# Linear attention with expert routing: subtracting the queries' maxima one round earlier, and three small reorderings

## The chip, the cores and the metric

The kernel runs on one core of one Trainium2 chip. Its time is the device time of one execution in microseconds (us), given as the median of three executions. A profiled execution gives the trace from which every row below is taken; its times are counted from its first instruction. Engines are written as in the profile: PE is TensorE, PEld its weight loads, DVE is VectorE, ACT is ScalarE, POOL is GpSimd, SP is SyncE, which here issues most DMA transfers.

## The reference

Three blocks follow one another: linear attention, a mixture of eight experts with one expert per token, and a dense block.

```python
proj = x @ w_phi                                    # x is q or k: 4 batches, 8 heads, 576 rows, 64 wide
proj = proj - max(abs(proj), axis=-1)               # 128 features
phi  = concat(exp(proj), exp(-proj))
kv   = einsum('bhsf,bhsd->bhfd', phi(k), v);  z = phi(k).sum(over s)
attn = (phi(q) @ kv) / (phi(q) @ z + 1e-6)          # then to x: 2304 tokens x 512

e    = argmax(normalised(x) @ normalised(expert_emb).T / tau)
x    = gate[e] * (relu(x @ w1[e]) @ w2[e])          # experts 512 -> 1024 -> 512

h    = max(x @ m1, x @ m2, x @ m3)                  # 512 -> 768
out  = h @ w_out                                    # 2304 x 512
```

All is float32.

## The kernel before, in words

The order of the work on every engine is the order in which the code is written; an engine takes its instructions strictly one after the other and waits where one of them lacks its input or its buffer.

**Attention** (function `attention`) goes in 18 rounds, r0 to r17, and a tail. Keys come in 18 steps of up to 256 rows of four heads; queries in 16 portions v (half a batch's rows, four heads each, two units u of two heads per portion). A round holds pieces of several of them, each at another stage:

- `q_front(v)`: PE projects the queries of a portion into `psqf` (L331), ACT copies them to `pq` (L335), POOL takes the maximum over the 128 partitions, `partition_all_reduce`, into `mq` (L337). Two units, so two of each; POOL's is called PAR below.
- `q_exp(u)`: DVE subtracts `mq` from `pq` (L341), ACT takes the two exponentials into `ex` (L343, L344). It belongs to the portion of the round before.
- `k_proj`, `k_T`, `k_exp` for the next key step: products into `pskp` (L212), transposes into `pskT` with ACT's copy `kT` (L203), then per half DVE's maximum `mk` (L223) and subtraction `pk` (L225) and ACT's two exponentials `kp` (L226, L227).
- `q_T`: transposes of a later portion (`psqT`), DVE's copies `qT` (L319).
- `xwork`: for finished tokens, transposes `psxd` (L388) and `psx` (L405) and DVE's scaling `x` (L418).
- `k_acc`: products with the values into `kv` (L264), and the sums `z` (L269), which for a full step take `zr`, DVE's sum of two halves of `kp` made by `k_pair` (L236) at the end of the round before. `k_fin` closes a batch (`kvT` L276, `psz` L287, `pskv` L300).
- `q_num`, `q_den`: numerators `psn` (L363) and denominators `psd` (L378), DVE's copy `dn` (L380).

PSUM banks for the products and transposes come from one pool of five, handed out in turn (`bank`): a transpose late in a round waits until the reader of an earlier tile, for example DVE's `pk` or ACT's `kT`, has let its bank go. Portion v is projected in round r1 for v = 0 to r8 for v = 7, and in r10 to r17 for v = 8 to 15; r9 has no `q_front`.

**The tail** computes the routing: `Routing.blocks` makes one-hot rows `R` in three groups (L647), PE turns them into the token list `rt_tok` (L704), DVE copies it to `s2t` (L715), and POOL gathers the tokens of the first expert block from `x_d` by it (L868). The last rows of `x_d` are scaled and stored in between (`x_put`, L418 and L419). Two products per group keep PE at work (`warm`, L657).

**The experts** (`Moe`) and **the dense block** (`Moe2`) come after; no line of theirs is changed.

Of the kernel before, what the change touches and what calls it, by code (L numbers as in the profile page):

```python
# [11 lines left out]
I32 = mybir.dt.int32  # L12
AF = mybir.ActivationFunctionType
ALU = mybir.AluOpType
# [32 lines left out]
def attention(tc, q, k, v, w_phi, expert_emb, tau, x_d, lraw, ssq, ident, io, late, rt, ids):  # L47
# [6 lines left out]
    nc = tc.nc  # L54
    B, H, S, D = q.shape
    NF = w_phi.shape[1]
    E = expert_emb.shape[0]
    P = 128
    NT = B * S // P
    NP_ = H // 2  # L60
    SH = S // 2
    QR = SH // 4
    DH = D // 2
    NV = 4 * B
    LEAD = 4

    with ExitStack() as ctx:
# [67 lines left out]
        w2 = cp.tile([P, NF], F32, tag="w2", name="w2")  # L135
# [96 lines left out]
        def k_pair(n):  # L232

            if n < NS and steps[n][2] is not None:
                zr[n] = wk.tile([P, 4, 2 * NF], F32, tag="zr", name=f"zr{n}", bufs=1)
                nc.vector.tensor_tensor(zr[n], kp[n][:, :, 0], kp[n][:, :, 1], op=ALU.add)  # L236
# [69 lines left out]
        qT, pq, mq, ex, ot, dn, xs = {}, {}, {}, {}, {}, {}, {}  # L306
# [14 lines left out]
        def q_front(v):  # L321

            m, g = divmod(v, 2)
            for pp in range(2):
                u = m * NP_ + 2 * g + pp
                d = wk.tile([P, 2, SH], F32, tag="pq", name=f"pq{u}", bufs=4)
                psb = [bank(f"psqf{u}_{a}")[:, 0:SH] for a in range(2)]
                for j in range(2):
                    for a in range(2):
                        x = slice(a * D, (a + 1) * D)  # L330
                        nc.tensor.matmul(psb[a][:, j * 2 * QR:(j + 1) * 2 * QR], w2[x],  # L331
                                         qT[v][x, 2 * pp + j].rearrange("p b s -> p (b s)"), start=True, stop=True)
                dv = d.rearrange("p j (b a s) -> p j b a s", b=2, a=2)
                for a in range(2):
                    nc.scalar.copy(dv[:, :, :, a, :], psb[a].rearrange("p (j b s) -> p j b s", j=2, b=2))  # L335
                mx = wk.tile([P, 2, SH], F32, tag="mq", name=f"mq{u}", bufs=3)
                nc.gpsimd.partition_all_reduce(mx.rearrange("p a b -> p (a b)"), d.rearrange("p a b -> p (a b)"), P, ReduceOp.absmax)  # L337
                pq[u], mq[u] = d, mx

        def q_exp(u):  # L340
            nc.vector.tensor_tensor(pq[u], pq[u], mq.pop(u), op=ALU.subtract)  # L341
            e = wk.tile([P, 2, 2, SH], F32, tag="ex", name=f"ex{u}", bufs=10)
            nc.scalar.activation(e[:, 0], pq[u], AF.Exp)  # L343
            nc.scalar.activation(e[:, 1], pq[u], AF.Exp, scale=-1.0)  # L344
            ex[u] = e
# [91 lines left out]
        for b in range(B):  # L437
            lst = [pc for pc in pcs if pc[1] == b]
            for i, (n, bb, lo, hi) in enumerate(lst):
                r = max(n, done.get(b - 1, n))  # L440
# [5 lines left out]
        at = {r: qd for qd, r in back.items()}  # L446
# [23 lines left out]
        k_proj(0)  # L470
        for _ in k_exp(0):
            pass
        k_pair(0)
        fin = None
        for r in range(R1):

            if r + LEAD in at:
                q_front(at[r + LEAD])
            if r + LEAD - 1 in at:
                m, g = divmod(at[r + LEAD - 1], 2)  # L480
                for pp in range(2):
                    q_exp(m * NP_ + 2 * g + pp)
            k_proj(r + 1)

            k_T(r + 2)
            ke = k_exp(r + 1)
            next(ke, None)
            if r and r + LEAD + 1 in at:
                q_T(at[r + LEAD + 1])
            for _ in ke:  # L490
                pass
            if fin is not None:
                for _ in fin:
                    pass
                fin = None
            if xwork:
                if next(xwork[0], "end") == "end":
                    xwork.pop(0)
                    if xwork:
                        next(xwork[0])  # L500
            for _ in pe if r == 2 else ():
                pass

            pl = work.get(r, [])
            ends = [pc[1] for pc in pl if pc[5]]
            for pc in pl:
                if not ends or pc[1] == ends[0]:
                    k_acc(*pc)
            if r < NS:
                load_next(r)  # L510
            if ends:
                fin = k_fin(ends[0])
                next(fin)
            if r in at:
                m, g = divmod(at[r], 2)
                for pp in range(2):
                    q_num(m * NP_ + 2 * g + pp)
                if fin is not None:
                    next(fin)
                if g == 1:  # L520
                    q_den(m)
                    xwork.append(tiles(m))
            elif fin is not None:
                next(fin)
            for pc in pl:
                if ends and pc[1] != ends[0]:
                    k_acc(*pc)
            k_pair(r + 1)
            if r == 0:
                q_T(at[LEAD + 1])  # L530
            if r == 7:
                rt.token_ids(ids, QR)
            if r == R1 - 3:
                late(1)
            if r == R1 - 1:
                late(3)
# [22 lines left out]
        chain = rt.blocks(lambda nm: ps1.tile([P, free[0][1]], F32, tag=free.pop(0)[0], name=nm), bank)  # L559
# [7 lines left out]
        next(chain)  # L567
        xb = [(t, rv, x_out(t)) for t, rv in rb]
        x_put(*xb[0], act=True, dma=nc.scalar, sq=False)
        for x in xb[1:]:  # L570
            next(chain)
            x_put(*x, dma=nc.sync, sq=False)
        for _ in chain:
            pass
        for t in tb:
# [13 lines left out]
class Routing:  # L589
# [83 lines left out]
    def blocks(self, bank, wbank):  # L673

        nc, gp, rp, P, NT, E, NB = self.nc, self.gp, self.rp, 128, self.NT, self.E, self.NB
        V = nc.vector
        pet = [P, E, NT]
        t_ = lambda shape, nm, dt=F32: self.tmp(rp, shape, nm, dt)
        oh = self.oh
        inc = self.inc = self.tmp(gp, pet, "inc")  # L680
        V.tensor_tensor_scan(inc.rearrange("p e t -> p (e t)"), self.d0.rearrange("p e t -> p (e t)"),
                             oh.rearrange("p e t -> p (e t)"), 0.0, op0=ALU.mult, op1=ALU.add)
        ps = bank("rt_n")
        nc.tensor.matmul(ps[:, 0:E], self.ones, inc[:, :, NT - 1], start=True, stop=True)
        ps2 = bank("rt_before")
        nc.tensor.matmul(ps2[:, 0:E], self.tri, inc[:, :, NT - 1], start=True, stop=True)
        yield

        nb = t_([P, E], "nb")
        V.tensor_scalar(nb, ps[:, 0:E], 1.0, (P - 1) / 2, op0=ALU.max, op1=ALU.add)  # L690
        V.tensor_scalar(nb, nb, ROUND * P, -ROUND * P, op0=ALU.add, op1=ALU.add)
        cb = self.cb
        V.tensor_tensor_scan(cb[:, 1:], self.o8, nb, 0.0, op0=ALU.mult, op1=ALU.add)
        self.pos = self.places(rp, gp, cb, ps2[:, 0:E], "b")
        rf, bf = self.rows(rp, self.pos, "b")
        ohb = t_([P, NT, NB + 1], "ohb", F32R)
        full = [P, NT, NB + 1]
        V.tensor_tensor(ohb, bf.unsqueeze(2).to_broadcast(full), self.jb.unsqueeze(1).to_broadcast(full), op=ALU.is_equal)
        V.tensor_tensor(ohb, ohb.bitcast(F32), self.tid.unsqueeze(2).to_broadcast(full), op=ALU.mult)

        ps3 = bank("rt_tok")
        for group in self.one_hots(rp, rf, "R", (6, 6, 6)):
            for t, R in group:
                nc.tensor.matmul(ps3[:, 0:NB + 1], R, ohb[:, t, :], start=(t == 0), stop=(t == NT - 1))  # L704
            if t < NT - 1:
                self.warm(wbank, WARM[3])
            yield

        eb = t_([1, NB, E], "eb")
        V.tensor_tensor(eb, self.jb[0:1, 0:NB].unsqueeze(2).to_broadcast([1, NB, E]),  # L710
                        cb[0:1, 1:].unsqueeze(1).to_broadcast([1, NB, E]), op=ALU.is_ge)
        ebs = t_([1, NB], "ebs")
        V.tensor_reduce(ebs, eb, axis=AX.X, op=ALU.add)
        self.s2t = self.tmp(gp, [P, NB], "s2t", I32)
        V.tensor_copy(self.s2t, ps3[:, 0:NB])  # L715

        self.before = self.tmp(gp, [P, E], "before")
        V.tensor_copy(self.before, ps2[:, 0:E])
        ne = t_([P, E], "ne")
        V.tensor_copy(ne, ps[:, 0:E])  # L720
        self.ebi = self.tmp(gp, [1, NB], "ebi", I32)
        V.tensor_scalar(self.ebi, ebs, float(E - 1), None, op0=ALU.min)
        self.nbi = self.tmp(gp, [1, 1], "nbi", I32)
        V.tensor_scalar(self.nbi, cb[0:1, E:E + 1], 1.0 / P, None, op0=ALU.mult)
        V.tensor_tensor_scan(self.cn[:, 1:], self.o8, ne, 0.0, op0=ALU.mult, op1=ALU.add)
        yield
# [567 lines left out]
```

## Time and profile before

| | us |
|---|---|
| median of 3 runs | 824.07 (823.74 to 824.57) |
| profiled execution, time | 823.43 |
| its span, first to last instruction | 821.5 |
| PE busy | 780.2 (95%) |
| DVE busy | 520.5 (63%) |
| ACT busy | 450.2 (55%) |
| POOL busy | 162.6 (20%) |

The profiled execution's time is its span and 1.9 us around it. Attention and its tail take the first 222 us; the first expert block starts its products near 229 us, and from 260 us on PE is busy nearly without a break. So a microsecond saved ahead of 222 us is a microsecond of the whole, if the end of attention moves with it. Busy shares alone hide what happens inside a round, since every engine works on each round for a part of it: there one reads which instruction each engine waits for, and what ended the wait.

### The profile page before, as it was taken

The numbers are of one execution on the slowest core, as the hardware profiler recorded it, in microseconds if no ns is written. First come the engines' busy times: TensorE is split into PE (matmuls) and PEld (weight loads), VectorE is DVE, ScalarE is ACT, GpSimd is POOL, SyncE is SP. The second block draws the span as 40 slices with busy tenths as digits, with TensorE's granted clock in tenths as the row PEclk, the third lists the DMA queues.
The fourth block names the chain that finished last, engine by engine and source line by source line (L and its number), as shares of the span: only waits on it lengthen the run. The fifth ranks groups of instructions, "written<-read, shape, count | busy, mean of one in ns | idle before, by whom it ended". The sixth has DMA issues, their size and how long they took to land. (4 is left out here: it accounts for less than half of the span.)

```text
span 821.5 us, 14129 instructions
## 1 busy us (share of the span) xinstructions
PE 780.2 (95%) x5617; PEld 655.3 (80%) x5617; DVE 520.5 (63%) x673; ACT 450.2 (55%) x622; POOL 162.6 (20%) x117
## 2 busy tenths in 40 slices
PE   6889898889899999999999999999999999999996
PEld 4656565655678888888888787999989999899984
DVE  7666666766799999999888897888212222122210
ACT  3676656666678888888887895454221112211111
POOL 2554223442151121110332021000130002200001
PEclk9899999999999999999999999999999999999999
DMA  8534432025234347534654543452121001200001
GB/s 200 122 84 105 108 91 73 15 79 201 74 104 169 122 150 276 214 141 161 228 187 153 206 142 104 160 177 75 38 81 36 1 1 39 77 1 1 0 26 52
DMA packets 61988, 87.82 MB, mean 107 GB/s; under 512 B 9488, under 2 KB 39832, under 8 KB 61920
## 3 DMA queue, kind: packets, MB, share of 16 engines
q1 hardware_dynamic: 53392, 64.51, 24.7%
q0 software_dynamic: 4880, 15.99, 5.9%
q10 hardware_dynamic: 3648, 6.38, 2.1%
q8 instruction: 46, 0.75, 0.4%
q14 instruction: 22, 0.18, 0.1%
HBM read 129.59 MB, written 16.00 MB: 177 GB/s over the span
## 5 line engine op out<-in xcount | busy, mean ns | idle before, releaser
L898 DVE TENSOR_TENSOR wL<-raw,wH 128x2048 fp32r<-128x2048 f32 x88 | 200.0, 2289 | 21.3 <-ACT wH L897 20.6
L897 ACT CAST wH<-raw 128x2048 fp32r<-128x2048 f32 x88 | 167.6, 1916 | 29.4 <-PE ph L924 12.9
L1125 PE MATMUL ps<-yH,m2WH 128*128 128x384 f32 x432 | 145.1, 336 | 1.3 <-ACTq L1261 1.3
L1125 PE MATMUL ps<-yH,m2WL 128*128 128x384 f32 x432 | 145.0, 336 | 0.0
L1125 PE MATMUL ps<-yL,m2WH 128*128 128x384 f32 x432 | 145.0, 336 | 0.0
L337 POOL PARTITION_ALL_REDUCE mq<-pq x32 | 71.3, 2274 | 109.2 <-ACT pq L335 109.2
L1125 PEld LDWEIGHTS ps<-yH,m2WH 128*128 128x128 f32 x432 | 81.2, 188 | 1.8 <-ACTq L1261 1.7
L1133 ACT CAST h2H<-mm 128x384 fp32r<-128x384 f32 x36 | 18.5, 515 | 115.6 <-DVE mm L1130 115.6
L1125 PEld LDWEIGHTS ps<-yL,m2WH 128*128 128x128 f32 x432 | 81.2, 188 | 0.1
L1125 PEld LDWEIGHTS ps<-yH,m2WL 128*128 128x128 f32 x432 | 81.2, 188 | 0.0
L1079 POOL DMA_INDIRECT yg<-ys,c2s x18 | 24.8, 1378 | 247.4 <-PE psyT L1094 222.6
L868 POOL DMA_INDIRECT xs<-x_d,s2t x22 | 42.3, 1923 | 153.5 <-PE psxT L907 90.1
L956 PE MATMUL py<-wH,hH 128*128 128x512 f32 x176 | 70.4, 400 | 0.4 <-ACT hH L942 0.4
L956 PE MATMUL py<-wH,hL 128*128 128x512 f32 x176 | 69.2, 393 | 0.1
L956 PE MATMUL py<-wL,hH 128*128 128x512 f32 x176 | 68.8, 391 | 0.0
L1129 DVE TENSOR_TENSOR mm<-mm,ps 128x384 f32<-128x384 f32 x36 | 19.9, 553 | 74.5 <-PE ps L1125 74.3
L924 PE MATMUL ph<-wH,xH 128*128 128x512 f32 x176 | 56.5, 402 | 0.7 <-ACT xH L910 0.7
L924 PE MATMUL ph<-wH,xL 128*128 128x512 f32 x176 | 54.7, 392 | 0.2 <-DVE xL L911 0.2
L924 PE MATMUL ph<-wL,xH 128*128 128x512 f32 x176 | 54.5, 391 | 0.0
L1130 DVE TENSOR_TENSOR mm<-mm,ps 128x384 f32<-128x384 f32 x36 | 20.0, 555 | 43.4 <-PE ps L1125 43.4
L1147 ACT ACTIVATE ot<-pso,gatec 128x512 f32<-128x512 f32 x18 | 12.4, 689 | 60.2 <-PE pso L1145 32.9
L1148 POOL DMA_INDIRECT out_dram<-ot,c2t x18 | 17.7, 983 | 132.3 <-ACT ot L1147 128.6
(214 smaller groups left out, 1428.3 us busy)
## 6 DMA issues: line engine op xcount, KB each, us to landing
raw<-in_moe_w_dram SPq DMA_DIRECT2D x88, 1024.0 KB
wr<-in_moe_w_dram SPq DMA_DIRECT2D x18, 512.0 KB
ys<-y ACTq DMA_DIRECT2D x22, 256.0 KB
q<-in_q_dram SPq DMA_DIRECT2D x8, 576.0 KB
kv<-in_v_dram SPq DMA_DIRECT2D x8, 512.0 KB
x_d<-x SPq DMA_DIRECT2D x16, 256.0 KB
kv<-in_k_dram SPq DMA_DIRECT2D x7, 512.0 KB
wr<-in_moe_w_out_dram SPq DMA_DIRECT2D x6, 512.0 KB
```

What stands on the lines that cost most here:

```text
L337: nc.gpsimd.partition_all_reduce(mx.rearrange("p a b -> p (a b)"), d.rearrange("p a b -> p (a b)"), P, ReduceOp.absmax)
L868: nc.gpsimd.indirect_dma_start(out=d, out_offset=None, in_=self.x_d, in_offset=bass.IndirectOffsetOnAxis(ap=self.s2t[:, j:j + 1], axis=0))
L897: nc.scalar.copy(wH, ex.raw[i])
L898: nc.vector.tensor_tensor(wL, ex.raw[i], wH.bitcast(F32), op=ALU.subtract)
L924: nc.tensor.matmul(ph[:, n * 512:(n + 1) * 512], a[:, cs], w[:, c * DF + n * 512:c * DF + (n + 1) * 512], start=(kc == 0 and f == 0), stop ...
L956: nc.tensor.matmul(py, a[:, cs], w[:, ws], start=(fc == 0 and q == 0), stop=(fc == 7 and q == 2))
L1079: self.nc.gpsimd.indirect_dma_start(out=d, out_offset=None, in_=self.ys[0:rows, :], in_offset=bass.IndirectOffsetOnAxis(ap=self.rt.c2s[:, ...
L1125: nc.tensor.matmul(ps, w[:, c], y[:, k], start=(k == 0 and q == 0), stop=(k == NK - 1 and q == 2))
L1129: nc.vector.tensor_tensor(m, m, pss[1], op=ALU.max)
L1130: nc.vector.tensor_tensor(m, m, pss[2], op=ALU.max)
L1133: nc.scalar.copy(hH[:, f], m)
L1148: nc.gpsimd.indirect_dma_start(out=self.out, out_offset=bass.IndirectOffsetOnAxis(ap=self.rt.c2t[:, t:t + 1], axis=0), in_=o, in_offset=None)
```

## The change

- The subtraction of the maxima leaves `q_exp` and becomes `q_sub(v)`. It runs in the round that projected the portion, behind that round's `k_exp`, `fin` and `xwork`, instead of at the head of the next round.
- `k_pair(0)`, which stood ahead of the rounds, runs in r0 behind `k_exp(1)`; and in r0 the `q_T` of the first portion now comes ahead of `k_pair(1)`.
- In `q_front`, two products of 144 columns per array half and unit become one of 288.
- In the tail, all three one-hot groups come ahead of the second `x_put`, the copy to `s2t` comes ahead of the third, and the two products that only kept PE at work between the groups go.

```diff
-                for j in range(2):
-                    for a in range(2):
-                        x = slice(a * D, (a + 1) * D)
-                        nc.tensor.matmul(psb[a][:, j * 2 * QR:(j + 1) * 2 * QR], w2[x],
-                                         qT[v][x, 2 * pp + j].rearrange("p b s -> p (b s)"), start=True, stop=True)
+                for a in range(2):
+                    x = slice(a * D, (a + 1) * D)
+                    nc.tensor.matmul(psb[a], w2[x], qT[v][x, 2 * pp:2 * pp + 2].rearrange("p j b s -> p (j b s)"),
+                                     start=True, stop=True)
...
+        def q_sub(v):
+            m, g = divmod(v, 2)
+            for pp in range(2):
+                u = m * NP_ + 2 * g + pp
+                nc.vector.tensor_tensor(pq[u], pq[u], mq.pop(u), op=ALU.subtract)
+
         def q_exp(u):
-            nc.vector.tensor_tensor(pq[u], pq[u], mq.pop(u), op=ALU.subtract)
...
-        k_pair(0)
         fin = None
         for r in range(R1):
...
             for _ in pe if r == 2 else ():
                 pass
+            if r == 0:
+                k_pair(0)
+            if r + LEAD in at:
+                q_sub(at[r + LEAD])
...
-            k_pair(r + 1)
             if r == 0:
                 q_T(at[LEAD + 1])
+            k_pair(r + 1)
...
-        for x in xb[1:]:
-            next(chain)
-            x_put(*x, dma=nc.sync, sq=False)
+        next(chain)
+        next(chain)
+        x_put(*xb[1], dma=nc.sync, sq=False)
+        next(chain)
+        x_put(*xb[2], dma=nc.sync, sq=False)
...
-            if t < NT - 1:
-                self.warm(wbank, WARM[3])
             yield
+        self.s2t = self.tmp(gp, [P, NB], "s2t", I32)
+        V.tensor_copy(self.s2t, ps3[:, 0:NB])
+        yield
...
-        self.s2t = self.tmp(gp, [P, NB], "s2t", I32)
-        V.tensor_copy(self.s2t, ps3[:, 0:NB])
```

On DVE at the start, from the second half of key step 0 to the end of r0. Before:

```order
L223 TENSOR_REDUCE mk_1_224<-pskp_1_208 128x4
L225 TENSOR_TENSOR pk_1_226<-pskp_1_208,mk_1_224 128x512
L236 TENSOR_TENSOR zr_230<-kp_217 128x1024
L223 TENSOR_REDUCE mk_0_250<-pskp_0_232 128x4
L225 TENSOR_TENSOR pk_0_252<-pskp_0_232,mk_0_250 128x512
L223 TENSOR_REDUCE mk_1_256<-pskp_1_233 128x4
L225 TENSOR_TENSOR pk_1_258<-pskp_1_233,mk_1_256 128x512
L236 TENSOR_TENSOR zr_285<-kp_249 128x1024
L319 COPY qT_289<-psqT_0_290 128x4x72
L319 COPY qT_289<-psqT_1_296 128x4x72
```

The same place in the changed kernel:

```order
L223 TENSOR_REDUCE mk_1_224<-pskp_1_208 128x4
L225 TENSOR_TENSOR pk_1_226<-pskp_1_208,mk_1_224 128x512
L223 TENSOR_REDUCE mk_0_248<-pskp_0_230 128x4
L225 TENSOR_TENSOR pk_0_250<-pskp_0_230,mk_0_248 128x512
L223 TENSOR_REDUCE mk_1_254<-pskp_1_231 128x4
L225 TENSOR_TENSOR pk_1_256<-pskp_1_231,mk_1_254 128x512
L236 TENSOR_TENSOR zr_260<-kp_217 128x1024
L319 COPY qT_287<-psqT_0_288 128x4x72
L319 COPY qT_287<-psqT_1_294 128x4x72
L236 TENSOR_TENSOR zr_300<-kp_247 128x1024
```

The first pair sum stands behind the maxima and subtractions of step 1, and the second behind the copies of the first queries.

On DVE where r6 passes into r7 (`dn` is the copy of r6's denominators, the last `mk` belongs to r7). Before:

```order
L225 TENSOR_TENSOR pk_1_938<-pskp_1_898,mk_1_936 128x512
L380 COPY dn_991<-psd_992 128x288
L236 TENSOR_TENSOR zr_1010<-kp_914 128x1024
L341 TENSOR_TENSOR pq_867<-pq_867,mq_876 128x576
L341 TENSOR_TENSOR pq_878<-pq_878,mq_887 128x576
L223 TENSOR_REDUCE mk_0_1060<-pskp_0_1042 128x4
```

The same place in the changed kernel:

```order
L225 TENSOR_TENSOR pk_1_914<-pskp_1_874,mk_1_912 128x512
L343 TENSOR_TENSOR pq_849<-pq_849,mq_856 128x576
L343 TENSOR_TENSOR pq_858<-pq_858,mq_865 128x576
L384 COPY dn_969<-psd_970 128x288
L236 TENSOR_TENSOR zr_988<-kp_890 128x1024
L223 TENSOR_REDUCE mk_0_1032<-pskp_0_1014 128x4
```

The two subtractions of a portion have moved ahead of `dn` and `zr`, and nothing stands between `zr` and the next round's `mk` any more.

On PE, the queries' projection of one round (r7). Before:

```order
L331 MATMUL psqf_0_1013<-qT_923,w_85 128x144
L331 MATMUL psqf_1_1014<-qT_923,w_85 128x144
L331 MATMUL psqf_0_1013<-qT_923,w_85 128x144
L331 MATMUL psqf_1_1014<-qT_923,w_85 128x144
L331 MATMUL psqf_0_1024<-qT_923,w_85 128x144
L331 MATMUL psqf_1_1025<-qT_923,w_85 128x144
L331 MATMUL psqf_0_1024<-qT_923,w_85 128x144
L331 MATMUL psqf_1_1025<-qT_923,w_85 128x144
```

The same place in the changed kernel:

```order
L330 MATMUL psqf_0_991<-qT_899,w_85 128x288
L330 MATMUL psqf_1_992<-qT_899,w_85 128x288
L330 MATMUL psqf_0_1000<-qT_899,w_85 128x288
L330 MATMUL psqf_1_1001<-qT_899,w_85 128x288
L212 MATMUL pskp_0_1014<-w_85,kT_888 128x128
```

Four products of twice the columns stand for eight, with the first product of the next key step behind them; the two array halves still take turns.

## Rows read from the trace of the kernel before

**Rows 1.** Stretch totals: length, busy us (instructions) per engine, granted clock, DMA.

```profile
260.00:820.00 560.00, 550.55 (x2883) 494.18 (x2881) 334.27 (x323) 279.59 (x289) 70.79 (x51) 1.00 0.30 106
```

**Rows 2.** Stretch totals of the four stretches at a granted clock of 0.50.

```profile
20.04:23.45 3.41, 3.41 (x30) 3.41 (x32) 0.00 (x0) 1.40 (x4) 1.25 (x1) 0.50 0.95 212
33.69:37.10 3.41, 3.41 (x32) 1.78 (x36) 2.12 (x6) 2.99 (x6) 0.49 (x1) 0.50 0.39 79
125.85:129.26 3.41, 3.13 (x22) 1.80 (x26) 3.27 (x11) 2.83 (x6) 1.16 (x1) 0.50 0.00 0
183.88:187.29 3.41, 3.41 (x36) 1.70 (x32) 2.38 (x8) 1.88 (x4) 0.00 (x0) 0.50 0.03 11
```

**Rows 3.** Timeline, r0 into r1: start, us, engine, line, names, count, [idle before].

```profile
12.84 1.23 DVE L236 TENSOR_TENSOR zr<-kp 128x1024 f32<-128x1024 f32 x1 [1.22 <-ACT kp L227]
...
13.98 0.68 DVE L223 TENSOR_REDUCE mk<-pskp 128x4 f32<-128x512 f32 x1
...
15.29 1.22 PE L317 MATMUL psqT<-ident,q 72*128 72x72 f32 x8
15.31 0.68 DVE L223 TENSOR_REDUCE mk<-pskp 128x4 f32<-128x512 f32 x1
...
20.03 2.29 PE L331 MATMUL psqf<-qT,w 64*128 64x144 f32 x16 [3.52 <-DVE qT L319]
```

**Rows 4.** Timeline of r2, from the maxima to PE's wait.

```profile
29.16 5.02 POOL L337 PARTITION_ALL_REDUCE mq<-pq  x2 [2.65 <-ACT pq L335]
29.66 2.52 DVE L341 TENSOR_TENSOR pq<-pq,mq 128x576 f32<-128x576 f32 x2
...
33.65 0.54 PE L183 MATMUL ps_en<-ident,emb 8*128 8x8 f32 x4 [2.58 <-DVE pk L225]
```

**Rows 5.** Timeline of r4, PE's two waits.

```profile
46.76 1.16 PE L212 MATMUL pskp<-w,kT 64*128 64x128 f32 x14 [0.98 <-ACT pq L335]
...
53.16 1.02 PE L280 MATMUL z<-kvT,enp 128*32 128x256 f32 x8 [1.42 <-ACT kvT L276]
```

**Rows 6.** Timeline of r5, where no subtraction delays the round's head.

```profile
56.83 1.25 PE L331 MATMUL psqf<-qT,w 64*128 64x144 f32 x16
58.49 4.26 POOL L337 PARTITION_ALL_REDUCE mq<-pq  x2 [7.13 <-ACT pq L335]
...
60.70 0.41 PE L287 MATMUL psz<-ident,zs 128*128 128x128 f32 x2 [0.30 <-DVE pk L225]
...
61.83 1.09 PE L300 MATMUL pskv<-ident,kvT 128*128 128x128 f32 x8 [0.72 <-ACT kT L203]
```

**Rows 7.** Timeline of r7.

```profile
76.76 1.25 PE L331 MATMUL psqf<-qT,w 64*128 64x144 f32 x16
78.41 2.52 DVE L341 TENSOR_TENSOR pq<-pq,mq 128x576 f32<-128x576 f32 x2
82.40 0.41 PE L388 MATMUL psxd<-ident,dn 128*128 128x128 f32 x2 [2.07 <-DVE pk L225]
82.74 0.66 PE L405 MATMUL psx<-ident,oT 128*128 128x128 f32 x4
```

**Rows 8.** Timeline of r9, the round without a projection.

```profile
100.34 1.42 DVE L341 TENSOR_TENSOR pq<-pq,mq 128x576 f32<-128x576 f32 x2
...
103.23 0.41 PE L287 MATMUL psz<-ident,zs 128*128 128x128 f32 x2 [2.26 <-DVE pk L225]
```

**Rows 9.** Timeline of r11 and r16.

```profile
126.13 0.66 PE L388 MATMUL psxd<-ident,dn 128*128 128x128 f32 x2 [2.09 <-DVE pk L225]
...
177.04 1.25 PE L331 MATMUL psqf<-qT,w 64*128 64x144 f32 x16
...
182.68 0.63 PE L405 MATMUL psx<-ident,oT 128*128 128x128 f32 x4 [2.29 <-DVE pk L225]
```

**Rows 10.** Timeline of the hand-over to the experts.

```profile
219.62 0.68 DVE L418 TENSOR_TENSOR x<-psx,r 128x512 f32<-128x512 f32 x1
...
223.52 1.30 POOL L868 DMA_INDIRECT xs<-x_d,s2t  x1 [28.44 <-issue]
```

## The prediction

> **What bounds the kernel now.** I read the totals by stretch first. From 260 us to 820 PE is busy 550.55 of 560 us [rows 1]: nothing of the change lies there, and what attention and its tail lose ahead of 222 us is lost to the whole. Then I read the timeline of attention round by round, looking only for idle time in front of a PE instruction and for what ended it. A round with nothing in its way is r5: its projection starts at 56.83, the first transpose that needs a bank from DVE at 60.70, with 0.30 of idle, the one that needs ACT's `kT` bank at 61.83 [rows 6]. So a clean round has these two at +3.87 and +5.00. Against it the reader is to see three places. In r2, r7, r9, r11 and r16 the same kind of transpose waits 2.07 to 2.58 us for DVE's `pk` [rows 4, 7 to 9]. In each of these rounds the two subtractions of the queries' maxima stand ahead of the round's `mk` and `pk` on DVE; in r2 and r7 they also run beside POOL's PAR and take 2.52 instead of 1.42 us [rows 4, 7, 8]. At the start, PE idles 3.52 us before the first projection [rows 3]. And four stretches of 3.41 us have a granted clock of 0.50, that is 1.2 GHz [rows 2]; PE idled in front of each of them, by 3.52, 2.58, 2.09 and 2.29 us [rows 3, 4, 9].
>
> **The change part by part.**
>
> *First pair sums.* Before, DVE sits idle for 1.22 us, from 11.62, because `zr` of step 0 at 12.84 waits for ACT, and step 1's maxima stand behind it [rows 3]. Now step 1's two pairs of maximum and subtraction start at 11.62; a pair takes 15.31 - 13.98 = 1.33 us, two 2.7, and `zr` follows from 14.3 to 15.5 instead of 12.84 to 14.07. PE's `z` waits for it, so `psqT` behind `z` moves by the same 1.4, from 15.29 to 16.7 at the latest, and ends with its 1.22 us near 17.9 [rows 3]. DVE copies it at once, since the second `zr` no longer stands ahead of the copies, and the projection starts near 18.1 instead of 20.03. Gain 1.9. Bounds: 0, if the first queries or the later `z` hold all behind them; 3.5, if the whole idle goes.
>
> *Subtractions earlier.* They are the same 32 instructions, now queued in the round of their PAR. In a clean round PAR ends at 58.49 + 4.26 = 62.75, that is +5.92 [rows 6]; DVE has two `mk`, two `pk` and two `qT` copies to do until about then, so the first subtraction waits little. Behind the waiting instruction stand only `dn`, `zs` and `zr`, wanted by PE no sooner than the next round. So the move costs nothing as long as DVE has about 1.5 us to spare at the end of a round; without that cover it would cost up to the pair's 1.42 us per round. What goes, each a wait of PE:
> - r2: 2.58 of idle to the clean 0.30, gain 2.3.
> - r4: 0.98 for ACT's `pq` and 1.42 for `kvT` [rows 5], both because ACT runs late after exponentials that waited for the subtractions. ACT has little to spare in these short rounds, so I take 1.0; bounds 0 and 2.4.
> - r7: the first transpose could start at 76.76 + 3.87 = 80.63 instead of 82.40, but next is `psx`, which waits for ACT's `kT` bank: 76.76 + 5.00 = 81.76 instead of 82.74 [rows 6, 7]. Gain 1.0, not 1.8: ACT is late next.
> - r9: 100.34 loses its 1.42 us pair, less the overlap of some 0.1; gain 1.3 [rows 8].
> - r11 repeats r7 (2.09 for 2.07): 1.0 [rows 9].
> - r16 has no `kT`, so the transpose itself counts: 177.04 + 3.87 = 180.91 instead of 182.68 [rows 6, 9], gain 1.8.
> - The other rounds are clean already; nothing. Sum of the six: 8.4.
>
> *The clock.* With the idle in front of the four slow stretches gone or shortened I expect the full clock there. The prices: the first projection took 2.29 us, a clean one 1.25 [rows 3, 7], 1.0. The other three cost at most half of PE's busy time in them: 1.7, 1.6 and 1.7 [rows 2]. I take 1.4, 1.3 and 1.6, a little less, since PE had to wait for other engines in them too. Sum 5.3; bounds 0 (slow stretches fall elsewhere instead) and 6.0 (1.0 and the three halves).
>
> *One product per half.* Columns are the same: per unit and half 2 x 144 against 288. The eight products of a round stand as 16 instructions in 1.25 us [rows 7]; now eight, with half the weight loads, which lie beside the products anyway. I take 0. Bounds: +0.15 per round saved, 2.4 in 16 rounds, if an eighth of the 1.25 is cost per instruction; a loss of 1.0 per round, 16 in all, if the halves stopped overlapping.
>
> *Tail.* The last `x_put` started at 219.62 and the gather at 223.52, after that row had been stored [rows 10]. The `R` group ahead of it now comes earlier, but it also stands behind `s2t`, which waits for PE's token list. I take 0.3 earlier; bounds -0.5 and 1.0. Fewer products that only keep PE at work could cost clock at the hand-over, at most half of a stretch like those in [rows 2], 1.7.
>
> *Sum.* 1.9 + 8.4 + 5.3 + 0 + 0.3 = 15.9. The profiled execution took 823.43, 1.9 around its span of 821.5, so 807.5 for an execution like it. The median of the runs is 0.64 above that execution: 808.2.
>
> **Rivals.**
>
> *The clock is not given back.* The waits go, but slow stretches come elsewhere in attention, whose PE remains idle here and there. For it: r7 and r9 idled as long (2.07, 2.26) without one, so where they fall is not fixed by the wait alone [rows 7, 8]. Against it: after the change no wait over about 1.5 us is left between r1 and r17. 808.2 + 5.3 = 813.5.
>
> *The first rounds are bound by everything at once.* r1 to r4 are the shortest rounds, and PAR, DVE and ACT each have a full portion and a full key step in them; with the waits gone, `zr` slips into the next PAR and ACT runs late. Then r0, r2 and r4 give nothing (1.9 + 2.3 + 1.0), nor does the clock in r1 and r2 (2.4): 808.2 + 7.6 = 815.8. Against it: each of these waits has one named cause that the change takes away.
>
> *The halves stop overlapping.* 16 us of loss: 824.2, no change. Against it: a product already stands as two instructions on one half, and the halves take turns as before.
>
> *Every round's subtraction meets its PAR* (slower). The pair took 2.52 instead of 1.42 where it met a PAR, and that pair of PARs 5.02 instead of 4.26 [rows 4, 6, 8]: 1.10 + 0.76 = 1.86 us. If DVE came to the subtraction with PAR still running in all 16 rounds and had no slack, 16 x 1.86 = 29.8 would come on top: 808.2 + 29.8 = 838.0; it makes the kernel measurably slower from 1.1 us per round on, (825.7 - 808.2) / 16. For it: at +5.92 PAR ends just as DVE arrives. Against it: what is left of PAR then is a few tenths, and in rounds with `xwork` DVE arrives later still.
>
> The Trainium skill, SBUF — State Buffer, section "Who interferes with whom", says that a DVE instruction with two SBUF inputs contends with a GpSimd instruction that reads SBUF, and that the one which issues second is blocked for the whole of the other. By that rule a subtraction that comes early would wait for all of what is left of a PAR of 2.13 us, 16 x 2.13 = 34 us at most and a time of 842 at the far end. The trace agrees that they contend, but has 1.10 us for the delay, not 2.13 [rows 4, 8].
>
> **How the numbers follow.** Forecast, with the clock given back in most places: 0.62, own range 804.5 to 812. Clock not given back: 0.15. First rounds give nothing: 0.13. Halves: 0.05. Collisions: 0.05. A range from 804.5 to 815.5 takes in the forecast with what may still come on top (the merged products' 2.4, 1.0 of the tail), the clock rival and, nearly, the first rounds' case, and leaves out the last two and the far ends of the terms. About 0.2%, 1.6 us, is what a measurement of this kernel can tell from no change. Faster by more than that: 0.91. Within: 0.04, most of the halves' case. Slower: 0.05.
>
> **What would show it.** In the changed profile: the first projection near 18 us; r2 without an idle of over 0.5 in front of `ps_en`; the first transposes of r7, r11 and r16 near +3.9 and `psx` waiting for ACT's `kT`; every pair of subtractions near 1.5 us and none at 2.5; a granted clock of 1.00 where the four stretches stood; r5's start near 49 instead of 56.83; attention's end some 15 us earlier and from there to the end the same length as before. It is wrong if the eight projection instructions of a round take over 1.4 us, if `zr` makes PE wait in r1 to r4, or if as many slow stretches remain as there were.

## The result, and the profile after

The changed kernel takes 811.17 us (median of four executions, 809.54 to 815.09), the kernel before, beside it on the same chip, 824.32 (823.74 to 824.65). The ratio is 0.9848 with a 95% interval of 0.9812 to 0.9884, a gain of 13.2 us where 15.9 were forecast. The profiled execution took 811.43 with a span of 809.4, 12.0 and 12.1 less than before. The two traces run 11.7 us apart from the first expert's products on, and 12.1 from 483.0 us of the kernel before on: 0.4 of the 12.1 comes at one step inside the experts (481.6 to 483.0), and the trace of attention and its tail must hold the 11.7.

The timeline of the changed kernel first, in the places of [rows 3 to 10]. Columns: start, us, engine, line, operation, names, count, and in brackets the idle time before it and what ended that. The subtraction is now L343, the projection L330.

```profile
15.24 0.89 PE L269 MATMUL z<-zr,ones 128*32 128x256 f32 x8 [1.76 <-DVE zr L236]
...
17.84 2.29 PE L330 MATMUL psqf<-qT,w 64*128 64x288 f32 x8 [0.55 <-DVE qT L319]
25.25 1.42 DVE L343 TENSOR_TENSOR pq<-pq,mq 128x576 f32<-128x576 f32 x2
...
25.40 1.24 PE L330 MATMUL psqf<-qT,w 64*128 64x288 f32 x8
29.41 0.38 PE L183 MATMUL ps_en<-ident,emb 8*128 8x8 f32 x4 [0.30 <-DVE pk L225]
...
45.75 1.44 PE L280 MATMUL z<-kvT,enp 128*32 128x256 f32 x8 [1.42 <-ACT kvT L276]
47.12 3.64 PE L264 MATMUL kv<-kp,vr 64*32 64x256 f32 x32
...
73.24 1.24 PE L330 MATMUL psqf<-qT,w 64*128 64x288 f32 x8
77.11 0.41 PE L392 MATMUL psxd<-ident,dn 128*128 128x128 f32 x2 [0.30 <-DVE pk L225]
78.23 0.66 PE L409 MATMUL psx<-ident,oT 128*128 128x128 f32 x4 [0.71 <-ACT kT L203]
...
99.34 0.66 PE L409 MATMUL psx<-ident,oT 128*128 128x128 f32 x4 [0.74 <-DVE pk L225]
...
168.83 1.24 PE L330 MATMUL psqf<-qT,w 64*128 64x288 f32 x8
172.69 0.63 PE L409 MATMUL psx<-ident,oT 128*128 128x128 f32 x4 [0.52 <-DVE pk L225]
...
181.32 1.86 DVE L343 TENSOR_TENSOR pq<-pq,mq 128x576 f32<-128x576 f32 x1 [1.27 <-POOL mq L336]
183.44 0.76 DVE L343 TENSOR_TENSOR pq<-pq,mq 128x576 f32<-128x576 f32 x1 [0.27 <-POOL mq L336]
...
207.98 0.68 DVE L422 TENSOR_TENSOR x<-psx,r 128x512 f32<-128x512 f32 x1
211.87 1.30 POOL L876 DMA_INDIRECT xs<-x_d,s2t  x1 [28.47 <-issue]
```

Every wait for DVE's `pk` of over 2 us is gone: r2's idle is 0.30 instead of 2.58, r7's transpose starts at +3.87 and `psx` behind it waits for ACT's `kT` at +4.99, r9 has no such wait left for `psz` and only 0.74 for a `psx`, r16's stands at +3.86. Fifteen of the 16 pairs of subtractions take 1.41 to 1.44 us; the last, in r17, waits for its PAR and runs beside it, 1.86 and 0.76. Two things are new. At the start PE now waits 1.76 us for `zr` ahead of `z`, where it did not wait before. In r4 the wait for `kvT` is the 1.42 us it was [rows 5], but the 32 products behind it take 3.64 us, where the same products in a round at full clock take 1.93.

The stretch totals of the changed kernel say why. Columns: stretch and length, then busy us (instructions) of PE, PEld, DVE, ACT and POOL, the granted clock, DMA share and GB/s.

```profile
15.50:22.33 6.83, 6.28 (x43) 4.86 (x36) 2.51 (x4) 1.40 (x4) 2.30 (x2) 0.50 0.97 231
...
46.22:49.63 3.41, 3.41 (x30) 1.26 (x32) 1.56 (x2) 0.00 (x0) 0.00 (x0) 0.50 0.03 5
49.63:53.04 3.41, 3.41 (x32) 1.48 (x25) 0.00 (x0) 0.00 (x0) 0.00 (x0) 0.50 0.00 0
53.04:56.46 3.42, 3.42 (x25) 2.92 (x22) 0.04 (x1) 2.37 (x6) 1.84 (x1) 0.50 0.00 0
...
210.06:213.47 3.41, 3.41 (x18) 3.41 (x18) 0.51 (x1) 2.56 (x4) 1.30 (x2) 0.50 0.04 16
```

The kernel before had two such stretches beside the four of [rows 2]:

```profile
13.21:16.62 3.41, 3.30 (x32) 1.55 (x23) 3.34 (x5) 1.22 (x3) 1.44 (x4) 0.50 0.88 158
221.42:224.84 3.42, 3.42 (x17) 3.42 (x18) 0.24 (x1) 2.82 (x4) 1.30 (x1) 0.50 0.13 50
```

From 33.69, 125.85 and 183.88, where slow stretches stood [rows 2], the clock is now 1.00. But the one at the start is as long as the two that stood there together (13.21 and 20.04), and there is a new one of 10.24 us in r4 and r5, in which PE is busy all the time. Before the experts the trace before had 20.5 us at half rate, six stretches of 3.41 or 3.42 us; the trace after has 6.83 + 10.24 + 3.41 = 20.5 as well.

The starts of the projections, read from the timelines of both kernels, put the gain into rounds (r8 and r9 together, since r9 has no projection; rounds that differ by 0.01 or less are left out):

| round | length before | length after | gain | forecast, wait + clock |
|---|---|---|---|---|
| start to r1's projection | 20.03 | 17.84 | 2.19 | 1.9 |
| r1 | 7.10 | 7.56 | -0.46 | 0 + 1.0 |
| r2 | 10.73 | 6.61 | 4.12 | 2.3 + 1.4 |
| r3 | 6.11 | 5.77 | 0.34 | 0 |
| r4 | 12.86 | 14.61 | -1.75 | 1.0 |
| r5 | 10.26 | 11.19 | -0.93 | 0 |
| r7 | 10.81 | 9.81 | 1.00 | 1.0 |
| r8 and r9 | 22.44 | 21.11 | 1.33 | 1.3 |
| r11 | 12.13 | 9.80 | 2.33 | 1.0 + 1.3 |
| r16 | 12.12 | 8.66 | 3.46 | 1.8 + 1.6 |
| r17 to the first expert's transpose | 38.33 | 38.28 | 0.05 | 0.3 |

They add up to 11.7. All rows but those of r1, r4 and r5, where the clock went down, come within 0.5 of the forecast.

### The profile page after: what moved, and what is told of

The parts are those of the page before. It is cut to its first block, busy times and chain, and to the rows that moved or that the text cites. A ratio compares the mean times of both kernels' runs of the same rounds, so it can differ in the third digit from the quotient of the medians.

```text
span 809.4 us, 13863 instructions
## 1 busy us (share of the span) xinstructions
PE 778.3 (96%) x5485; PEld 651.4 (80%) x5485; DVE 516.1 (64%) x673; ACT 448.9 (55%) x622; POOL 162.1 (20%) x117
## 5 line engine op out<-in xcount | busy, mean ns | idle before, releaser
L336 POOL PARTITION_ALL_REDUCE mq<-pq x32 | 69.1, 2207 | 101.0 <-ACT pq L334 101.0
```

## The experiments

Each of e1 to e4 makes one part of the change alone in the kernel before (824.68 us beside them, 29 executions).

**e1, the subtractions alone.**

```
+        def q_sub(v): ...                       # as in the change
         def q_exp(u):
-            nc.vector.tensor_tensor(pq[u], pq[u], mq.pop(u), op=ALU.subtract)
...
             for _ in pe if r == 2 else ():
                 pass
+            if r + LEAD in at:
+                q_sub(at[r + LEAD])
```

> The kernel before with the subtractions of the maxima moved to the end of their round, and nothing else. Theory (each wait of PE for pk in r2, r7, r9, r11, r16 came from the subtractions in front of it; the half-rate stretches only move): the waits go as in the changed kernel, 8.4 us, and the slow stretches stay about as long in sum as before: 816, between 813 and 818, with psxd of r7 at +3.9 after the projection. Rival (the full clock comes back with the waits, so another part of the change brought the slow stretch of r4 and r5): 811.6. Rival (the subtraction gains only together with the earlier start of r1): over 820.

812.35 us, ratio 0.9864 (0.9831 to 0.9896). Nearly the whole gain is in this part. The theory's 816 missed and the first rival's price, 811.6, came: e1 gains 12.3 us, 3.9 more than the forecast for the waits. Its profiled execution has 10.24 us at half rate before the experts, not 20.5, and its six executions have a mean clock of 0.987 on average against 0.981 for the kernel before beside them, so part of the clock seems to have come back with the waits. That another part of the change brings the slow stretch in r4, as the rival has it, doesn't follow; e12 below has all the parts and no such stretch in its trace. The profiled execution, mean clock 0.991, has no slow stretch in r4 either, though the wait there is the same; the rows are PE's of r4:

```profile
40.60 1.25 PE L331 MATMUL psqf<-qT,w 64*128 64x144 f32 x16
...
48.57 1.02 PE L280 MATMUL z<-kvT,enp 128*32 128x256 f32 x8 [1.42 <-ACT kvT L276]
49.52 1.93 PE L264 MATMUL kv<-kp,vr 64*32 64x256 f32 x32
...
52.25 1.01 PE L331 MATMUL psqf<-qT,w 64*128 64x144 f32 x12
```

So r4 takes 52.25 - 40.60 = 11.65 at full clock, 1.2 less than before, and the changed kernel's 14.61 is 2.96 of half rate on top; r5, 10.25 here and 11.19 there, adds 0.94.

**e2, one product per half alone.**

```
-                for j in range(2):
-                    for a in range(2):
-                        ...            # 144 columns each
+                for a in range(2):
+                    ...                # 288 columns
```

> The kernel before with one product of 288 columns per array half and unit, and nothing else. Theory (columns decide): 824.3, between 823.5 and 825, the eight instructions of a round in 1.24 us. Rival (cost per instruction): 822. Rival (halves overlap less): 830 and more, with the instructions of a round in over 1.4 us.

825.47, ratio 1.0021 (0.9994 to 1.0049): no difference that can be told from the noise. A round's products take 1.24 us in the changed kernel against 1.25 [rows 7].

**e3, the first pair sums alone.**

```
-        k_pair(0)
...
+            if r == 0:
+                k_pair(0)
...
-            k_pair(r + 1)
             if r == 0:
                 q_T(at[LEAD + 1])
+            k_pair(r + 1)
```

> The kernel before with the first pair sums later, and nothing else. Theory: the first projection comes 2 us earlier (near 18 instead of 20.0), but the half-rate stretch there stays or comes earlier with it: 822.4, between 821 and 823. Rival (the start is given back in r2 and r4, where DVE and ACT run late anyway): 824. Rival (clock comes back too): 821.

822.35, ratio 0.9967 (0.9947 to 0.9988), a gain of 2.3 us. The first projection starts at 17.65 instead of 20.03 and still takes 2.29 us, at half rate, as the theory had it.

**e4, the tail alone.**

```
-        for x in xb[1:]:
-            next(chain)
-            x_put(*x, dma=nc.sync, sq=False)
+        next(chain)
+        next(chain)
+        x_put(*xb[1], dma=nc.sync, sq=False)
+        next(chain)
+        x_put(*xb[2], dma=nc.sync, sq=False)
...
-            if t < NT - 1:
-                self.warm(wbank, WARM[3])
...                                       # s2t earlier, as in the change
```

> The kernel before with the changed order of the routing at the end of attention, and nothing else. Theory: the gather starts 0.3 us earlier: 824.0. Rival (the two products left out cost clock at the hand-over): 825 to 826, with a second half-rate stretch near 222 us.

824.51, ratio 1.0004 (0.9973 to 1.0035): nothing that can be measured. The last `x` and the gather are 3.89 us apart after the change (207.98 and 211.87, and 221.02 and 224.91 in e4) and were 3.90 apart before [rows 10]. The gather waits for that row to be stored, so what stands ahead of it doesn't count.

**e8, everything but the subtractions** (before 824.39 beside it).

```
-        def q_sub(v): ...
         def q_exp(u):
+            nc.vector.tensor_tensor(pq[u], pq[u], mq.pop(u), op=ALU.subtract)
```

> The changed kernel without its main part: the subtractions stand in the next round again; first pair sums, merged products and tail as changed. If the parts add up, as e1 to e4 alone suggest (pair sums -2.3, merged products +0.8 and tail -0.2, both within their uncertainty), it takes 821.5 to 823, and the waits of 2.1 to 2.6 us for DVE's pk in r2, r7, r9, r11 and r16 are back. Rival (the other parts only pay once the subtractions are out of the way, or the other way round): under 819 or over 825.

822.83, ratio 0.9974 (0.9948 to 1.0000), and the long waits are back; r2's on PE:

```profile
31.60 0.46 PE L183 MATMUL ps_en<-ident,emb 8*128 8x8 f32 x4 [2.58 <-DVE pk L225]
```

The parts add up, as closely as these measurements tell (the intervals reach 1.7 to 2.7 us to either side): 12.3 + 2.3 + 0.2 - 0.8 = 14.0 alone, 13.2 together; the three small ones make 1.7 alone and 1.6 here.

**e6, the changed kernel once more** (before 824.41 beside it and e5, e7 and e9).

> The changed kernel itself once more, for where its half-rate stretches fall in another profile. Theory (their places change from run to run, as the spread of its four times, 809.5 to 815.1, and of the kernel before, 820.4 to 830.9, has it): 811.5, the runs spread over 4 us or more, and the profile has its slow stretches at other places than 15.5 and 46.2 us, or fewer of them. Rival (they are fixed by the kernel): the same two places.

812.45 (808.88 to 817.17), ratio 0.9843 (0.9803 to 0.9882). The slow stretches stand at the same places, 6.83 us from 16.08 and 10.24 from 46.80, so for this profile the rival holds and not the theory; e12 below shows them elsewhere. The six executions fall in order with their mean clock: 808.88 at 0.991 down to 817.17 at 0.982.

**e5, work in r4's wait.** Six calls of products that only keep PE at work (twelve in the trace) right in front of the product that waits for `kvT`.

```
             if ends:
                 fin = k_fin(ends[0])
                 next(fin)
+                if r == 4:
+                    rt.warm(bank, 6)
```

> The changed kernel with six products that only keep PE at work in r4, ahead of the products that wait 1.42 us for kvT; the output is the same. Theory (the wait in r4 brought the 10.2 us at a granted clock of 0.50 from 46.2 on, and that stretch costs up to 5.1 us): no half-rate stretch between 42 and 60 us, r4 as long as at full clock or 0.3 longer, and a time of 807 to 808 beside 811 for the changed kernel. Rival (the slow stretch comes from the work itself, 32-column products of 64 rows): the stretch stays and the time is 811. Rival (the clock only moves on to the next wait): 811, with slow stretches elsewhere between 60 and 200 us.

807.04 (804.51 to 812.21), ratio 0.9791 (0.9753 to 0.9828). All three forecasts of the theory came. The rows of PE in r4: the wait is filled, the products behind it run at full clock, r4 takes 11.65 us.

```profile
45.11 1.60 PE L668 MATMUL warm<-onesq 128*128 128x128 f32 x12
46.64 0.98 PE L280 MATMUL z<-kvT,enp 128*32 128x256 f32 x8
47.55 1.93 PE L264 MATMUL kv<-kp,vr 64*32 64x256 f32 x32
```

I took this for the proof that the wait of 1.42 us brings the slow stretch. The next experiments speak against it. Nor is the clock all that differs between executions: four of e5's six have the same mean clock of 0.989 and take 806.75, 807.16, 811.54 and 812.21. What makes up these 5 us is not shown, since only one of them has a trace.

**e7, e5 with such work in r0 too.**

```
+        def fill(n): ...          # n products of wz into the bank "warm"
...
+            if n == 0:
+                fill(6)           # ahead of the first kv products
...
+                fill(6)           # ahead of the first pair sums' products
```

> As the kernel with six more products in r4, and twice six more in r0, where PE waits 1.7 us ahead of the first kv products and 1.8 ahead of the first sums; the output is the same. Theory (the half-rate stretches at the start follow PE's waits there): none between 13 and 23 us or half as much, 1 to 2 us less than with r4 alone: 806. Rival (the start is too short of work to hold the full clock, or the additional products delay the sums): 808.

809.09 (806.10 to 811.83), ratio 0.9795 (0.9764 to 0.9827): no better than e5, nearer the rival's 808 than the theory's 806. In its trace the first projection does run at full clock, 1.24 us from 18.20, but PE then waits 3.77 us, up to 30.89, for a transfer of `q` and a slow stretch stands behind that.

**e10, e5's products at the end of r3, where PE waits for nothing** (before 824.39). In the trace no numerators stand in r3: the products come right ahead of r4's projection.

```
+            if r == 3:
+                rt.warm(bank, 6)
             if ends:
                 fin = k_fin(ends[0])
```

> The changed kernel with the same twelve 128-column products that e5 puts in front of r4's wait, now in r3, ahead of its numerators, where PE waits for nothing. Theory (e5 gained because its products stand in the 1.42 us wait for kvT, so that PE isn't idle there): these cost their own 1.3 us in r3, the wait of 1.42 in r4 stays, a stretch at half rate follows it as in the changed kernel; 812 to 814. Rival (e5 gained because anything that shifts r4 in time makes the slow stretch miss it): no slow stretch between 42 and 60 us, 808 to 810.

807.94 (806.83 to 812.68), ratio 0.9822 (0.9794 to 0.9850). The rival's price came, not the theory's 812 to 814. The theory behind e5 falls with PE's rows of r4: the wait is there, nearly whole, and the clock behind it is full.

```profile
37.17 1.61 PE L668 MATMUL warm<-onesq 128*128 128x128 f32 x12
...
46.30 1.11 PE L280 MATMUL z<-kvT,enp 128*32 128x256 f32 x8 [1.33 <-ACT kvT L276]
47.34 1.93 PE L264 MATMUL kv<-kp,vr 64*32 64x256 f32 x32
```

**e11, small products in r3 instead, and e12, e10's products in r6** (before 824.10).

```
+            if r == 3:                                   # e11
+                ps = bank("warm")
+                for i in range(20):
+                    c = 32 * (i % 4)
+                    nc.tensor.matmul(ps[c:c + 32, 0:2 * NF], ones[0:D, 0], wz.bitcast(F32)[0:D], ...)
...
+            if r == 6:                                   # e12
+                rt.warm(bank, 6)
```

> The changed kernel with twenty extra products in r3 at the place of e10's, but of the small kind that the sums z use (64 rows, 32 columns of weights, 256 columns moved, 16 of them 1.04 us), so about 1.3 us of them too. e10 left r4's wait of 1.33 us in place and had no slow stretch behind it. If the full-width products of e5 and e10 raised the clock's level by their kind, these don't: a slow stretch of 10 us behind r4's wait, mean clock near 0.985, 812 to 814. If any work or any shift of that length in r3 does, the stretch is gone as in e10: mean clock 0.99 or more, 807 to 809.

> The changed kernel with the same twelve full-width products as e5 and e10, but in r6, behind the slow stretch. If they work only where they stand just ahead of the stretch or in its wait, r4 is as in the changed kernel, half rate for 10 us, and the products cost their own 1.3 us: 812.5 to 814. If e5's and e10's gain has nothing to do with the place (a chance of the build or of the hour), r4 is free of it here too, in most executions: 808 to 810.

e11: 811.38 (807.62 to 815.98), ratio 0.9841 (0.9806 to 0.9877). e12: 812.35 (807.76 to 817.04), ratio 0.9862 (0.9829 to 0.9895). By the medians both lean to "only full-width products close ahead of the stretch help". The traces are less clear. First r4's products and stretch in e11, whose twenty small ones cost 2.36 us and not 1.3:

```profile
37.37 2.36 PE L522 MATMUL warm<-wz,ones 64*32 64x256 f32 x40
...
47.35 1.46 PE L280 MATMUL z<-kvT,enp 128*32 128x256 f32 x8 [1.42 <-ACT kvT L276]
```

```profile
46.96:57.20 10.24, 9.85 (x76) 5.32 (x78) 1.56 (x2) 2.21 (x7) 0.96 (x1) 0.50 0.01 2
```

Then e12, where nothing ahead of r6 differs from the changed kernel:

```profile
47.31 1.02 PE L280 MATMUL z<-kvT,enp 128*32 128x256 f32 x8 [1.42 <-ACT kvT L276]
48.27 1.93 PE L264 MATMUL kv<-kp,vr 64*32 64x256 f32 x32
```

```profile
47.00:57.00 10.00, 8.66 (x102) 5.84 (x102) 5.20 (x12) 5.80 (x14) 4.26 (x2) 1.00 0.11 28
```

Its slow stretches ahead of r6 are others than the changed kernel's: 6.83 us from 8.89 and 3.41 from 29.37.

The same instructions with the same wait of 1.42 us are followed by 10.24 us at half rate in the changed kernel, in e6 and e11, and by none in e1 and e12. So the wait alone doesn't decide it: it differs between executions. In half of e11's executions the clock is 0.994 or more and the time 807.62 to 808.91, in two it is 0.98 and the time over 815. e5's and e10's medians are 3 to 5 us below those of the changed kernel, e6, e11 and e12, but the intervals of e10 and the changed kernel overlap, and only e5's and e12's come apart, by a hair. Whether the full-width products raise the odds of a full clock in r4, and by what, stays open. e5 has the lowest median of all that ran.

**e9, the subtractions still earlier**, between the two halves of the round's key exponentials, so that DVE comes to them while PAR is running, and waits.

```
             ke = k_exp(r + 1)
             next(ke, None)
...
+            if r + LEAD in at:
+                q_sub(at[r + LEAD])
             for _ in ke:
                 pass
```

> The changed kernel with the subtractions of the maxima still earlier: between the two halves of k_exp, where POOL's second PAR of the round is still running. This is the collision that the prediction named as the slower case. By the rows (a subtraction that meets a PAR takes 1.85 instead of 0.75 us, the PAR up to 0.4 more; the second subtraction waits for its PAR to end): DVE's second half of k_exp starts some 3 us later in each of the 16 rounds, ACT's exponentials with it, and rounds without slack get longer by 0.5 to 1.5 us: 820, between 815 and 828. If the subtraction is blocked for the whole of the other's instruction, single subtractions take over 2.5 us and it is 825 or more. Rival (all of it is hidden): 811.

837.10 (835.16 to 844.47), ratio 1.0152 (1.0111 to 1.0194): 25 us slower than the changed kernel beside it (e6). The theory's 820 (815 to 828) missed by 17. The time is near the 838.0 of the prediction's fourth rival, but that is chance, for the mechanism is another. The timeline of e9 in r4, r5 and r6, and in r9 (POOL's L336 is PAR):

```profile
45.74 4.26 POOL L336 PARTITION_ALL_REDUCE mq<-pq  x2 [3.98 <-ACT pq L334]
...
48.52 1.25 DVE L343 TENSOR_TENSOR pq<-pq,mq 128x576 f32<-128x576 f32 x1
50.04 0.76 DVE L343 TENSOR_TENSOR pq<-pq,mq 128x576 f32<-128x576 f32 x1 [0.27 <-POOL mq L336]
50.72 0.68 DVE L223 TENSOR_REDUCE mk<-pskp 128x4 f32<-128x512 f32 x1
51.43 0.69 DVE L225 TENSOR_TENSOR pk<-pskp,mk 128x512 f32<-128x512 f32 x1
52.16 0.63 ACT L226 ACTIVATE kp<-pk 128x512 f32<-128x512 f32 x1 [2.08 <-DVE pk L225]
53.21 1.05 ACT L276 COPY kvT<-kv 128x512 f32<-128x512 f32 x2
53.92 1.46 PE L280 MATMUL z<-kvT,enp 128*32 128x256 f32 x8 [3.54 <-ACT kvT L276]
55.31 3.64 PE L264 MATMUL kv<-kp,vr 64*32 64x256 f32 x32
...
62.82 4.26 POOL L336 PARTITION_ALL_REDUCE mq<-pq  x2 [12.81 <-ACT pq L334]
66.68 1.42 DVE L343 TENSOR_TENSOR pq<-pq,mq 128x576 f32<-128x576 f32 x2
...
72.80 1.24 PE L330 MATMUL psqf<-qT,w 64*128 64x288 f32 x8
...
74.46 4.26 POOL L336 PARTITION_ALL_REDUCE mq<-pq  x2 [7.38 <-ACT pq L334]
77.17 1.32 DVE L343 TENSOR_TENSOR pq<-pq,mq 128x576 f32<-128x576 f32 x1
78.75 0.76 DVE L343 TENSOR_TENSOR pq<-pq,mq 128x576 f32<-128x576 f32 x1 [0.27 <-POOL mq L336]
82.47 1.24 PE L330 MATMUL psqf<-qT,w 64*128 64x288 f32 x8
...
96.37 2.22 POOL L336 PARTITION_ALL_REDUCE mq<-pq  x1
96.50 1.85 DVE L343 TENSOR_TENSOR pq<-pq,mq 128x576 f32<-128x576 f32 x1
```

In r6 the first subtraction runs beside the second PAR, 1.32 us instead of 0.76, and the second subtraction waits for that PAR to end, and PE loses nothing: 82.47 - 72.80 = 9.67, 9.66 in the changed kernel. The same holds in r7, r10, r11, r15 and r16, to 0.01 us. Most of the time goes where a batch closes. In r4 `mk` and `pk` of the key step's second half stand behind the subtraction that waits for PAR, ACT sits idle 2.08 us for that `pk`, its copy `kvT` stands behind the two exponentials, and PE waits 3.54 instead of 1.42 us and goes on at half rate. The closing waits in r9, r13 and r17 are 2.62, 3.02 and 2.36 us; in the changed kernel r13's is 0.91 and the other two are below 0.8. r4, r5, r8, r9, r13 and r14 lose 15.5 us of the 21.0 by which r17's projection is late, r2 and r3 another 5.6 (PE waits there for `pk` and for ACT's `pq`, by 0.54 to 0.98, and r3 has 3.41 us at half rate). Of the 15.5 the longer closing waits themselves are 6.4. The rest is for the most part half rate behind them: these rounds have 17.1 us more of it than in the changed kernel, which by half of its length is an estimate of 8.5 at most. Before the experts the half-rate stretches add up to 40.9 us instead of 20.5.

The rows also show how a subtraction and a PAR meet. In r4 the pair of PARs ends at 45.74 + 4.26 = 50.00 and the subtraction at 48.52 + 1.25 = 49.77; in r6 they end at 78.72 and 78.49, in r9 at 98.59 and 98.35. In all 13 rounds of e9 where a subtraction is lengthened it ends 0.23 us before its PAR does, whether it started 1.48 us ahead of that end and took 1.25 or 2.09 ahead and took 1.85. Where it starts only 0.40 to 0.83 us ahead of the end, as in r5 (66.68, PARs to 67.08), it takes the usual 0.75. So it is not slowed throughout: its times are those of an instruction that is held up to one point of the PAR, by an estimate 0.23 + 0.75 = 1.0 us before the PAR's end, and then runs at its usual speed. The profile's spans on POOL are rough, so the point itself is uncertain.

The Trainium skill, SBUF — State Buffer, section "Who interferes with whom", says that a DVE instruction with two SBUF inputs and a GpSimd one that reads SBUF contend, and calls their shared port pair an exclusive lock, which the instruction that issues first has for its whole length. These traces agree that the second waits, but not for the whole of a PAR: the lengthened subtractions end before it does.

## Why the prediction was right, and where it was not

**The waits: right, in size too.** Forecast 8.4. r7, r9, r11 and r16 came out within 0.1 us of wait and clock together. r2 gave 4.12 for 3.7. r4 was right in size only: its wait for ACT's `pq` is gone, 1.2 at full clock for 1.0, but its wait for `kvT` stayed at 1.42. The prediction had both come from exponentials that waited for the subtractions; for `kvT` that was wrong. From its `pq` copies to `kvT` ACT works without a gap of over 0.15 us, 6.12 us before (46.33 to 52.45) and 6.16 after (38.88 to 45.04), so `kvT` comes earlier only by as much as PE's own work does. The 1.0, a value between two bounds, was near 1.2 by luck. The next late thing was named rightly in r7 (ACT's `kT`). That the move costs nothing on DVE held in 15 rounds with the pair at 1.41 to 1.44 us, and in r17, where DVE came too early and the pair took 1.86 + 0.76, no PE instruction waits for it; e9 shows what that cover is worth.

**First pair sums: right.** Forecast 1.9, 2.19 in the trace, 2.3 alone (e3). `z` did become later by its wait for `zr`, 0.98 us (14.26 to 15.24), where the sum allowed 1.4.

**One product per half, 0, and tail, 0.3: right within the noise.** e2 and e4 find nothing; the trace has 0.01 us a round, and 0.05 of the 0.3 at the tail.

**The clock: the term that failed.** The step was "with the idle in front of the four slow stretches gone or shortened I expect the full clock there", 5.3. In r2, r11 and r16 that held. At the first projection it did not: it took 2.29 us again. The idle in front of it had moved more than gone: 0.55 us is left there, and the 1.76 for `zr` stand ahead of it. And a new stretch in r4 and r5 took 2.96 + 0.94 = 3.9 us, against the argument that no wait over about 1.5 us would be left to bring one: the wait of 1.42 was enough, or was not needed. The total at half rate is the 20.5 us it was, so in this execution the clock gave back nothing net; that is the first rival, "the clock is not given back", 813.5, and the result of 811.17 stands between it and the forecast. Of the prediction's own signs of being wrong one thus came, by length as much slow time as there was, and r5 starts at 52.39 instead of near 49.

Over more executions part of the 5.3 may have come back: the mean clock is 0.985 on average in ten executions of the changed kernel (those of the result and e6), and 0.982 in the eleven of the kernel before beside e6. What was not granted is then 0.018 of some 822 us before and 0.015 of some 810 after, so by an estimate 2.6 us came back. The single values overlap (0.982 to 0.991, and 0.972 to 0.988), so this is not shown. The one execution of the changed kernel at a mean clock of 0.991 took 808.88 (e6). The forecast was thus the time of a good execution, and the mistake was to count as a sum what comes with a chance. The range of 804.5 to 815.5 held the forecast and this rival both, so that the result fell into it doesn't speak for the clock term.

**The other rivals.** The first rounds were not bound by everything at once: r2 gave all, and no `zr` held PE in r1 to r4. The halves overlap as before. The collision rival had its point of decision wrong: it spread the cost over all rounds. In six rounds of e9 the collision costs PE nothing; it is dear where the waiting instruction has the closing copy of a batch behind it, and less so in r2 and r3.

## What to carry to other kernels

Price a wait of PE by the round: where the same step stands free in a neighbouring round, the difference of the two, cut by whatever is late next, came out to a tenth of a microsecond in four of six rounds here. Do not add up what a returning clock would give for each slow stretch; give it a chance, and forecast the waits alone. And before an instruction that must wait is moved up in a queue, look for the rounds in which what stands behind it feeds the critical engine: they set the price, not the average round.

## What the runs showed of the hardware

- TensorE's granted clock stayed at 0.50 (1.2 GHz) for 10.24 us in which PE was busy throughout by the profile, at first with products of 32 columns and 64 rows, then with r5's projections and transposes (changed kernel, 46.22 to 56.46). The same instructions behind the same wait of 1.42 us ran at 1.00 in other executions (e1, e12). The Trainium skill, TensorE: Matmul & The Clock Gate, section "What's actually happening", says that the number of slow products at the start of a kernel differs from run to run; these traces show such differences behind the start too, at 46 us.
- Executions of one kernel spread with it, 808.88 to 817.17 in order of their mean clock, 0.991 to 0.982 (e6), but not with it alone: 806.75 to 812.21 at a mean clock of 0.989 (e5).
- A DVE subtraction of 128x576 with both inputs in SBUF takes 0.75 us alone and 1.25 to 1.86 where it starts 1.48 to 2.09 us ahead of the end of a PAR, and then ends 0.23 us before that end (e9). A pair of PARs took 4.26 us in e9's r4 with the subtractions beside it, as in a clean round [rows 6].
